# One transformer block on one core: loads on two queues, Wq transposes early, output buffers in turn, eleven numerator products, a new hand-off order

## The chip, the cores and the metric

The kernel runs on one core of one Trainium2 chip. The metric is the time of one execution on the device, in microseconds; the median of three runs of the kernel before is 277.59 us (277.17 to 278.16). One execution was also profiled: its own time is 276.56 us, and the span from its first to its last instruction is 274.8 us.

## The reference

The input x has 2048 rows of 640 values, in bfloat16. The block is an attention without a score matrix, followed by a gated product, each behind a layer norm and a residual.

```python
qkv = layernorm(x) @ wqkv                       # 640 x 1920; 32 heads of 20
pq, pk = q @ w_phi[head], k @ w_phi[head]       # 20 x 20 for each head
phi_q = concat(softmax(pq), softmax(-pq))       # 40 features a head; the same for phi_k
kv, z = phi_k^T v, sum over rows of phi_k       # one 40 x 20 block and 40 sums for each head
o = (phi_q kv) / (phi_q z + 1e-6)
h = x + o @ wo
g, u = layernorm(h) @ w_gate, layernorm(h) @ w_up   # 640 x 1536 each
out = h + (g * u) @ w_down                      # 1536 x 640
```

## The kernel before, in words

The 2048 rows are 16 tiles of 128 rows. All weights and all of x stay in the core's memory once loaded.

**What is computed in the beginning.** `Phi` is laid out as blocks (`Ph`). `w_phi` is folded into the K and Q weights: Wk is transposed by TensorE (`WT0..4`, line 391) and multiplied by `Phi` (`F1_0..4`, line 410). Wq is transposed by the DMA, straight from memory (`wqt0..4`, line 310: five transposes of 128x640), and multiplied by `Phi` (`F0_0..4`, line 410 again). A fold product of Wq needs all five transposes.

**For each row tile t.** Statistics of the row (`L1s`, `L1a`, lines 427 to 430), normalized rows (`xn`), their transpose (`xt`: by TensorE for tiles 0 to 3, line 461, by the DMA for the others, line 470). Then projections of ten 320-column products each: `V`, `K` and `Q` (line 483). `K` and `Q` go through two exponentials on ScalarE (`Kx`, `Qx`, line 495), a sum per head on VectorE (`Ks`, `Qs`, line 499), a reciprocal by ln and exp on ScalarE (`Kr`, `Ke`, lines 502 and 504) and a product on GpSimd (`Kn`, line 519, or `Qn`, line 550). `KV` (line 527) adds the tile to the sum over all rows. After all 16 `KV` the sums are masked (`KVe`), and for each tile follow the transposed features (`qT`, line 561), the numerators and denominators (`N`, line 575), the division (`dd`, `rd`, `o`, lines 586 to 591), the transpose of o (`oT`, line 595), the product with Wo (`O`, line 601), the residual (`h`, line 605), the second layer norm (`L2s`, `L2a`, `hc`) and its transpose (`hT`, line 628).

**The gated part** has row blocks of 256, 512, 512, 512 and 256 rows. `U` (line 643) is the product with the gate or up weights, `g` (line 648) moves the gate half from the accumulator, `u` (line 651) multiplies both, and `D` (line 662) is the product with the down weights. `y` (line 674) adds the residual, and `w` (line 676) writes the output.

**What sets the order.** Nothing is scheduled at run time. A table in the source, `PLAN` (lines 47 to 147), gives each operation a key, and where there is a choice an engine and a buffer slot; a planner outside the kernel wrote it from its own costs. `arrange` (line 685) sorts each engine's operations by the key, so an engine takes its operations in that order and waits at the first that is not ready. A semaphore wait of a DMA's issue also stands in that order. Loads and output writes are issued on SP's queue or on ScalarE's, by the second number of the entry; DMA transposes are always issued on SP.

**The loads before.** SP issues everything that the first tiles need, one after another: x0, w5, wk0, wk1, x1, wk2, x2, wk3, wk4, x3, wv1, wv0, wv2, x4, wv4, wv3, then x6 to x15. `PACE` (lines 307, 320 to 328 and 473) ties each of the five `wqt` to a transpose `xt` of tile 8 to 12, and all of Wo, Wd, Wgate and Wup to `xt15`: in `PLAN` they come at 27 to 51. Three of them, wg1, wu2 and wd0, are on ScalarE's queue.

**Other pieces that the change touches.** Ten warm-up products write one accumulator bank (lines 368 to 373). `N` uses eleven feature blocks of three heads (the last of two), into two banks that hold 16 heads each; block 5 has heads 15 to 17 and is cut in two, so there are twelve products. `out` has three buffers, but the plan gives slot 0 to nearly every `y`: at the end y14, y11, y10, y12 and y13 all have slot 0, and only y15_1 has slot 1.

Of the kernel before, what the change touches and what calls it, by code (L numbers as in the profile page):

```python
# [8 lines left out]
ALU = mybir.AluOpType  # L9
# [47 lines left out]
L1s5:11.357 L1a5:14.537 L1s6:13.607 L1a6:14.647 L1s7:12.177 L1a7:14.427 L1s8:19.637 L1a8:22.207 L1s9:16.397 L1a9:22.097 L1s10:14.757 L1a10:20.567
L1s11:15.577 L1a11:20.457 L1s12:25.657 L1a12:33.07 L1s13:30.22 L1a13:32.96 L1s14:29.4 L1a14:35.53 L1s15:33.18 L1a15:35.42 L1l0:4.311 L1e0:4.741
L1l1:8.905 L1e1:9.335 L1l2:10.717 L1e2:11.689 L1n2:12.199 L1n3:11.999 L1l4:14.996 L1e4:15.839 L1n4:16.349 L1n5:16.749 L1n6:16.149 L1n7:16.549
L1l8:23.514 L1e8:23.974 L1n8:24.884 L1n9:24.484 L1n10:24.684 L1n11:24.284 L1l12:35.85 L1e12:36.28 L1n12:37.279 L1n13:37.479 L1n14:36.879 L1n15:37.079  # L60
xn0:5.073::0 xt0:5.753::2 xte0:6.412 xn1:9.817::0 xt1:10.517::0 xte1:11.066 xn2:12.997::0 xt2:13.801::2 xte2:14.372 xn3:13.036:1:1 xt3:14.08::3
xte3:15.216 xn4:17.809:1:2 xt4:21.977 xn5:17.717::1 xt5:19.257 xn6:19.146:1:3 xt6:20.617 xn7:17.217::0 xt7:17.897 xn8:26.814:1:2 xt8:31.277
xn9:31.04::0 xt9:33.997 xn10:25.861:1:1 xt10:28.557 xn11:25.157::0 xt11:25.837 xn12:37.812::1 xt12:38.492 xn13:39.771:1:3 xt13:43.052 xn14:37.661:1:0
xt14:46.812 xn15:39.732::2 xt15:41.212 V0_0:9.115::2 V0_1:9.702 V0_2:10.245 V0_3:11.339 V0_4:11.611 Ve0:12.412::0 K0_0:8.004::4 K0_1:8.492 K0_2:9.973
K0_3:10.796 K0_4:11.067 Kx0_0:11.789::0 Kx0_1:13.749 Ks0:18.217::0 Kr0:20.483 Ke0:21.346 Kn0:21.706 KV0:30.148::6,7 V1_0:12.442::6 V1_1:12.714
V1_2:13.257 V1_3:13.529 V1_4:14.359 Ve1:16.562::1 K1_0:11.899::0 K1_1:12.171 K1_2:12.986 K1_3:14.631 K1_4:14.902 Kx1_0:15.939::1 Kx1_1:17.186
Ks1:20.677::1 Kr1:23.734 Ke1:24.698 Kn1:25.084 KV1:30.463 V2:16.564::2 Ve2:18.523::2 K2:15.206::4 Kx2_0:19.859::2 Kx2_1:20.723 Ks2:22.317::2
Kr2:24.848 Ke2:25.711 Kn2:27.443 KV2:32.137 V3:17.922::6 Ve3:28.648:1:6 K3:19.281::0 Kx3_0:21.496::3 Kx3_1:22.891 Ks3:23.737::3 Kr3:26.574 Ke3:27.527
Kn3:29.802 KV3:37.886 V4:24.714::0 Ve4:26.477:1:4 K4:27.431::0 Kx4_0:29.164::6 Kx4_1:30.411 Ks4:31.54::1 Kr4:33.14 Ke4:34.003 Kn4:34.52 KV4:38.201
V5:23.356::2 Ve5:27.677::5 K5:21.997::4 Kx5_0:24.074::4 Kx5_1:25.087 Ks5:27.228::0 Kr5:28.924 Ke5:31.658 Kn5:32.161 KV5:44.265 V6:28.789::2  # L70
Ve6:31.034::0 K6:26.073::4 Kx6_0:28.301::5 Kx6_1:29.788 Ks6:34::2 Kr6:35.61 Ke6:36.07 Kn6:37.679 KV6:44.581 V7:20.639::2 Ve7:22.267::3 K7:30.779::4
Kx7_0:32.407::0 Kx7_1:33.38 Ks7:35.64::0 Kr7:37.421 Ke7:39.621 Kn7:40.038 KV7:47.199 V8:36.527::0 Ve8:38.374::2 K8:35.169::4 Kx8_0:36.797::2
Kx8_1:38.997 Ks8:40.232::2 Kr8:42.181 Ke8:43.052 Kn8:44.756 KV8:48.873 V9:39.875::0 Ve9:41.652:1:4 K9:38.517::2 Kx9_0:40.724::3 Kx9_1:41.557
Ks9:42.403::3 Kr9:44.928 Ke9:46.895 Kn9:47.255 KV9:54.937 V10:42.907::2 Ve10:44.575:1:6 K10:41.233::4 Kx10_0:43.202::6 Kx10_1:44.305 Ks10:45.327::0
Kr10:47.045 Ke10:47.908 Kn10:49.614 KV10:56.611 V11:33.811::2 Ve11:37.06:1:1 K11:32.452::0 Kx11_0:34.153::1 Kx11_1:34.987 Ks11:38.312::1 Kr11:40.484
Ke11:41.347 Kn11:42.397 KV11:59.643 V12:55.253::0 Ve12:56.965:1:2 K12:45.526::2 Kx12_0:47.285::4 Kx12_1:48.118 Ks12:48.952::1 Kr12:50.6 Ke12:51.05
# [160 lines left out]
def build_graph():  # L237
# [66 lines left out]
    xload("sp", 6, 8, 5.8, also=["act"])  # L304


    PACE = {t: [] for t in range(NT)}

    def wqt(g, key):
        return G.op("sp", "wqt%d" % g, lambda e: e.dma_start_transpose(  # L310
# [589 lines left out]
```

## Time and profile before

| what | value |
|---|---|
| median of three runs | 277.59 us |
| the profiled execution's own time | 276.56 us |
| its span | 274.8 us |
| TensorE busy | 266.0 us, 97% of the span |
| VectorE, ScalarE, GpSimd busy | 172.3, 113.2 and 88.6 us |
| granted TensorE clock, mean | 0.999 |
| DMA, queue q1 (issued by SP) | 65888 packets, 26.15 MB, 44.8% of 16 engines |
| DMA, queue q10 (issued by ScalarE) | 688 packets, 1.28 MB, 1.9% |
| gated products, line 643 | 600 of them, 34% of the chain that ended last |
| projections, line 483 | 480 of them, 22% |

How to read it: busy time of TensorE counts a product until its result is out, so products that follow one another overlap in it; a row of a timeline such as "2.72 us for 20 products" gives the pace, 136 ns for 320 columns. The DMA share counts the time of packets on 16 engines. Idle time in front of an instruction is shown in brackets with what ended it.

### The profile page before, as it was taken

The page shows a single profiled execution, that of the slowest core. Times are in us where ns is not written, and L with a number is a line of the kernel's source. Part 1 is how long each engine was busy: PE and PEld are TensorE (multiplying, and loading weights), DVE is VectorE, ACT ScalarE, POOL GpSimd, SP SyncE. Part 2 cuts the span into 40 slices and gives each one's busy share as a digit, 9 for nine tenths or more (in the row PEclk, how much of TensorE's full clock was granted, in tenths as well). Part 3 has the DMA queues.
Part 4 walks back from the last instruction along what each step waited for, and adds up shares of the span by engine and source line. Part 5 has one row for each costly group of instructions (what it writes and reads, how often), then busy time and mean ns, then how long its engine had stood idle before and what let it go on. Part 6 is the DMA issues. An engine that isn't in the chain of part 4 may idle for free.

```text
span 274.8 us, 5227 instructions
## 1 busy us (share of the span) xinstructions
PE 266.0 (97%) x2119; PEld 176.7 (64%) x2119; DVE 172.3 (63%) x319; ACT 113.2 (41%) x240; POOL 88.6 (32%) x105
## 2 busy tenths in 40 slices
PE   7899999899999799999999999999999999999995
PEld 3676777677777587764455787665554467544773
DVE  5899999767789979987576337433365122323432
ACT  4899887678985444303242232003012310033000
POOL 7016999979998438240000000000000000000000
PEclk9999999999999999999999999999999999999999
DMA  6944758999689789867522100331002001100011
GB/s 167 317 144 95 98 110 174 302 294 341 141 147 176 146 141 186 163 74 160 52 47 49 26 0 2 84 50 48 25 2 48 0 0 50 52 0 2 24 48 57
DMA packets 66600, 27.77 MB, mean 101 GB/s; under 512 B 57744, under 2 KB 65296, under 8 KB 66576
## 3 DMA queue, kind: packets, MB, share of 16 engines
q1 hardware_dynamic: 65888, 26.15, 44.8%
q10 hardware_dynamic: 688, 1.28, 1.9%
q8 instruction: 17, 0.28, 0.4%
q14 instruction: 7, 0.06, 0.1%
HBM read 11.00 MB, written 2.62 MB: 50 GB/s over the span
## 4 chain that ended last, share of the span: by engine, by line
PE 84%; DMA 7%; DVE 4%; SPq 3%; issue 0%; DVEq 0%; ACT 0%
PE ps L643 34%; PE ps L483 22%; PE ps L662 17%; PE ps L601 7%; DMA xnT<-xn 3%; SPq L284 2%; PE ps L575 2%; DMA Wp<-in_A_wqkv_dram 2%; DMA scratch<-o 2%; DVE SR L499 2%; PE ps L527 1%; DMA out_dram<-Wp 1%; DVE o L591 1%; SPq L595 0%; DVE Wp L674 0%
## 5 line engine op out<-in xcount | busy, mean ns | idle before, releaser
L643 PE MATMUL ps<-xnT,Wgu 128*128 128x512 bf16 (+1 forms) x600 | 107.0, 336 | 1.2 <-DMA xnT<-xn 1.0
L643 PEld LDWEIGHTS ps<-xnT,Wgu 128*128 128x128 bf16 x600 | 58.0, 98 | 44.2 <-DVE ev L651 1.2
L648 ACT ACTIVATE gt<-ps 128x512 bf16<-128x512 f32 (+1 forms) x60 | 30.7, 512 | 101.9 <-PE ps L643 89.0
L483 PE MATMUL ps<-Wp,xnT 128*128 128x320 bf16 x480 | 69.0, 299 | 1.7 <-DMA xnT<-xn 1.3
L483 PEld LDWEIGHTS ps<-Wp,xnT 128*128 128x128 bf16 x480 | 45.2, 98 | 19.3 <-DMA xnT<-xn 1.8
L651 DVE TENSOR_TENSOR ev<-ps,gt 128x512 bf16<-128x512 f32 (+1 forms) x60 | 33.0, 577 | 37.6 <-PE ps L643 18.7
L662 PE MATMUL ps<-Wd,ev 128*128 128x320 bf16 (+2 forms) x396 | 53.2, 295 | 0.0
L499 DVE TENSOR_REDUCE SR<-ek 128x64 f32<-128x1280 bf16 x32 | 46.8, 1471 | 6.1 <-ACT ek L495 4.2
L495 ACT ACTIVATE ek<-ps 128x640 bf16<-128x640 f32 x64 | 43.3, 703 | 11.4 <-PE ps L483 10.1
L662 PEld LDWEIGHTS ps<-Wd,ev 128*128 128x128 bf16 x396 | 38.2, 98 | 14.9
L550 POOL TENSOR_TENSOR ph<-ek,SR 128x1200 bf16<-128x1200 bf16 x16 | 35.5, 2220 | 13.5 <-DMA scratch<-ph 7.4
L519 POOL TENSOR_TENSOR ek<-ek,SR 128x1280 bf16<-128x1280 bf16 x16 | 37.3, 2355 | 6.6 <-ACT SR L504 6.5
L674 DVE SCALAR_TENSOR_TENSOR Wp<-ps,rs,x_all 128x640 bf16<-128x640 f32 (+3 forms) x18 | 14.3, 805 | 35.5 <-PE ps L662 32.3
L615 POOL TENSOR_SCALAR ln<-mv 128x1 f32<-128x1 f32 x16 | 3.3, 209 | 87.2 <-DVE mv L614 87.2
L601 PE MATMUL ps<-Wo,scratch 128*128 128x320 bf16 x160 | 23.7, 299 | 0.2 <-DMA scratch<-o 0.2
L601 PEld LDWEIGHTS ps<-Wo,scratch 128*128 128x128 bf16 x160 | 15.3, 98 | 6.7 <-DVE ev L651 0.3
L605 DVE TENSOR_TENSOR x_all<-ps,x_all 128x640 bf16<-128x640 f32 x16 | 13.1, 816 | 3.7 <-PE ps L601 3.7
L624 ACT ACTIVATE xn<-x_all,mv 128x640 bf16<-128x640 bf16 x10 | 8.2, 825 | 16.5 <-DVE mv L614 16.5
L591 DVE TENSOR_TENSOR o<-ps,sm 128x640 bf16<-128x640 f32 x16 | 12.9, 814 | 1.5 <-DMA scratch<-o 1.0
L427 DVE BATCH_NORM_STATS2 st<-x_all 128x6 f32<-128x320 bf16 x16 | 7.7, 479 | 3.1 <-DMA x_all<-in_A_x_dram 3.0
L502 ACT ACTIVATE SR<-SR 128x64 f32<-128x64 f32 x32 | 8.1, 254 | 3.1 <-DVE SR L499 2.9
L575 PEld LDWEIGHTS ps<-KVm,scratch 128*128 128x128 bf16 x192 | 7.4, 98 | 2.9 <-DMA scratch<-ph 0.8
(54 smaller groups left out, 150.0 us busy)
## 6 DMA issues: line engine op xcount, KB each, us to landing
out_dram<-Wp SPq DMA_DIRECT2D x15, 160.0 KB, 1.8
x_all<-in_A_x_dram SPq DMA_DIRECT2D x6, 320.0 KB, 6.0
Wgu<-in_B_w_gate_dram SPq DMA_DIRECT2D x4, 384.0 KB, 7.5
Wgu<-in_B_w_up_dram SPq DMA_DIRECT2D x4, 384.0 KB, 8.5
Wd<-in_B_w_down_dram SPq DMA_DIRECT2D x3, 480.0 KB, 10.9
scratch<-in_A_wqkv_dram SPq DMA_DIRECT2D x5, 160.0 KB, 3.2
Wp<-in_A_wqkv_dram SPq DMA_DIRECT2D x5, 160.0 KB, 4.7
x_all<-in_A_x_dram SPq DMA_DIRECT2D x4, 160.0 KB, 3.4
```

The lines of the kernel that those rows point to most:

```text
L483: ins = e.matmul(pb(b, hb)[:, 0:320], lhsT=T["xnT"][:, NC - 1 - c, P * t:P * (t + 1)], rhs=T["Wp"][:, POS[kind], c, 320 * hb:320 * (hb + 1 ...
L495: G.op("act", "%sx%d_%d" % (nm, t, s), lambda e, s=s, b=b, ek=ek: e.activation(out=T["ek"][:, ek.slots[0], :].rearrange("p (b h s f) -> p ...
L499: G.op("dve", "%ss%d" % (nm, t), lambda e, ek=ek, sr=sr: e.tensor_reduce(out=T["SR"][:, sr.slots[0], 0, :], in_=T["ek"][:, ek.slots[0], :] ...
L519: G.op("pool", "Kn%d" % t, lambda e, ek=ek, sr=sr: e.tensor_tensor(out=T["ek"][:, ek.slots[0], :].rearrange("p (h f) -> p h f", f=DH), in0 ...
L550: e.tensor_tensor(out=o_[:, 0:10 * P].rearrange("p (g n) -> p g n", n=P)[:, :, 0:120].rearrange("p g (h f) -> p g h f", f=DH), in0=i_[:, 0 ...
L591: G.op("dve", "o%d" % t, lambda e, sm=sm, b=b, o=o: e.tensor_tensor(out=T["o"][:, o.slots[0], :].rearrange("p (b h d) -> p b h d", b=2, d= ...
L601: ins = e.matmul(pb(b, hb)[:, 0:320], lhsT=T["oT"][:, oT.slots[0], c, :], rhs=T["Wo"][:, c, 320 * hb:320 * (hb + 1)], start=(c == 0), stop ...
L643: ins = e.matmul(pb(b)[:, 0:n], lhsT=T["Wgu"][:, gu, c, P * ft:P * (ft + 1)], rhs=T["xnT"][:, NC - 1 - c, o0:o0 + n], start=(c == 0), stop ...
L648: G.op("act", "g%d_%d" % (bi, ft), lambda e, pg=pg, gt=gt, n=n: e.activation(out=T["gt"][:, gt.slots[0], 0:n], in_=pb(pg)[:, 0:n], func=AF ...
L651: o_ = G.op("dve", "u%d_%d" % (bi, ft), lambda e, pu=pu, gt=gt, hh=hh, ft=ft, n=n: e.tensor_tensor(out=T["hh"][:, hh.slots[0], ft, 0:n], i ...
L662: ins = e.matmul(pb(b, hb)[:, 0:w], lhsT=T["hh"][:, hh.slots[0], ft, P * tt:P * (tt + 1)], rhs=T["Wd"][:, ft, c0 + w * hb:c0 + w * (hb + 1 ...
L674: return e.scalar_tensor_tensor(out=o, in0=i0, scalar=T["rs2"][:, t:t + 1], in1=i1, op0=ALU.mult, op1=ALU.add)
```

## The change

- **Queues in the beginning.** ScalarE's queue now issues, ahead of its first arithmetic, x1, wk1, x12, wv4, x14, x8, x6, wv2, wu0, wd1, wd2 and wo0; then, between its first small operations, wu1, wg1, wo2, wd3, wg2, wg4, wg0, wd0 and wu2, and later wg3. SP issues w5, x0, wk0, x2, wk3, wk2, wk4, x3, wv1, wv0, wqt0, wv3, wqt4, x4, wqt1, wqt3, wqt2, x10, wu4 and wu3, and then the first transpose of a row tile.
- **`PACE` is gone.** The late weights and the `wqt` are no longer tied to an `xt`; their place comes from the table alone.
- **Order.** All five `F0` and the products Q0 to Q3 now stand right behind K3, V2, V3 and K2 on TensorE, ahead of KV0. In the kernel before, the first `F0` stood behind K10, and Q1 behind K13. The rest of the table is new too: with it `O14`, `N10`, `D0` and others change places, and Ph0 to Ph2 are all on GpSimd.
- **Buffers in turn.** The last outputs y14, y12, y11, y13, y10 and y15_1 have slots 0, 1, 2, 0, 1, 2; the buffers of `g`, `o` and others rotate likewise.
- **Numerators.** The two banks hold 18 and 14 heads, no block is cut, and `N` has eleven products instead of twelve. `dd`, `rd` and `o` work on 36 heads (720 columns) instead of 32 (640); the last four are not used.
- **Warm-up.** The first eight products write eight different banks.

```diff
-x0:0.7 w5:1.18:1 wk0:1.66:1 wv0:5.98:1 wk1:2.14 wv1:5.5 wk2:3.1:1 wv2:6.46:1 wk3:4.06 wv3:7.9 wk4:4.54:1 wv4:7.42:1 x1:2.62 x2:3.58 x3:5.02:1 x4:6.94
-x6:8.38 x8:9.34 x10:9.82 x12:10.3 x14:8.86 wqt0:32.637 wqt1:35.357 wqt2:29.917 wqt3:27.197 wqt4:39.852 wo0:44.412 wo2:45.852 wd0:45.168:1 wd1:51.052
+x0:1.18 w5:0.7:1 wk0:1.66:1 wv0:5.02:1 wk1:1.18:1 wv1:4.54 wk2:3.1:1 wv2:4.06 wk3:2.62 wv3:6.86 wk4:3.58:1 wv4:2.14 x1:0.7:1 x2:2.14 x3:4.06:1 x4:8.7
+x6:3.58:1 x8:3.1:1 x10:13.26 x12:1.66:1 x14:2.62:1 wqt0:5.5 wqt1:9.18 wqt2:11.9 wqt3:10.54 wqt4:7.34 wo0:5.98:1 wo2:7.96:1 wd0:13.577:1 wd1:5.02:1
+wd2:5.5:1 wd3:8.44:1 wg0:13.097:1 wu0:4.54:1 wg1:7.48:1 wu1:6.68:1 wg2:9.02:1 wu2:15:1 wg3:28.37:1 wu3:14.22 wg4:10.123:1 wu4:13.74 id0:0.9 gl0:1.2
...
     for g in range(NC):
-        PACE[8 + g].append(wqt(g, 10 * (8 + g) - 19))
-    PACE[15] += [wrows("wo", lambda: T["Wo"], "A_wo", wo_b[0:2], 0, 2, 328, 81), wrows("wo", lambda: T["Wo"], "A_wo", wo_b[2:5], 2, 5, 492, 81)]
+        wqt(g, 10 * (8 + g) - 19)
+    wrows("wo", lambda: T["Wo"], "A_wo", wo_b[0:2], 0, 2, 328, 41)
+    wrows("wo", lambda: T["Wo"], "A_wo", wo_b[2:5], 2, 5, 492, 44)
...
     for k in range(NWARM):
-        G.op("pe", "warm%d" % k, warm, 0.43 if k < 8 else 0.22, LT, [z_b], [wm_b], -90)
+        def warm(e, k=k):
+            o = T["PS"][:, 512 * k:512 * (k + 1)] if k < 8 else pb(wm_b)
+            return e.matmul(o, lhsT=T["zero"][:, 0:P], rhs=T["zero"][:, :], start=True, stop=True)
...
-            for o_ in PACE[t]:
-                o_.before.append(G.by["xt%d" % t])
...
             for g in range(NB):
-                for h0, h1 in [(3 * g, 3 * g + BH[g])] if g != 5 else [(15, 16), (16, 18)]:
-                    y = h0 // 16
-                    ins = e.matmul(pb(b, y)[:, 21 * (h0 - 16 * y):21 * (h1 - 16 * y)], lhsT=T["phT"][:, phT.slots[0], g, :],
+                y, h0, h1 = g // 6, 3 * g, 3 * g + BH[g]
+                ins = e.matmul(pb(b, y)[:, 21 * (h0 - 18 * y):21 * (h1 - 18 * y)], lhsT=T["phT"][:, phT.slots[0], g, :],
...
-            in1=smv(sm, 1).unsqueeze(3).to_broadcast([P, 2, 16, DH]), op=ALU.mult), dve_c(640, True), LD, [b, sm], [o], kk)
+            in1=smv(sm, 1).unsqueeze(3).to_broadcast([P, 2, 18, DH]), op=ALU.mult), dve_c(720, True), LD, [b, sm], [o], kk)
```

More of the change, by code (lines that the diff above doesn't have):

```diff
@@ L48 @@
 for _t in """
-x0:0.7 w5:1.18:1 wk0:1.66:1 wv0:5.98:1 wk1:2.14 wv1:5.5 wk2:3.1:1 wv2:6.46:1 wk3:4.06 wv3:7.9 wk4:4.54:1 wv4:7.42:1 x1:2.62 x2:3.58 x3:5.02:1 x4:6.94
-x6:8.38 x8:9.34 x10:9.82 x12:10.3 x14:8.86 wqt0:32.637 wqt1:35.357 wqt2:29.917 wqt3:27.197 wqt4:39.852 wo0:44.412 wo2:45.852 wd0:45.168:1 wd1:51.052
-wd2:50.092 wd3:46.332 wg0:42.572 wu0:49.132 wg1:42.572:1 wu1:44.892 wg2:49.612 wu2:43.825:1 wg3:48.652 wu3:48.172 wg4:50.572 wu4:45.372 id0:2.41
-gl0:0.7 eps:0.95 id1:2.93 gla0:3.77 glb0:4.21 gla4:2.19 glb4:3.33 gla1:1.97 glb1:3.55 gla2:4.43 glb2:4.85 gla3:2.71 glb3:3.99 va1:1.15 phz:6.025
@@ L57 @@
[L57 to L64, printed above, removed]
@@ new lines @@
+F1_4:11.437::2 Fe1_4:12.473:1 L1s0:4.903 L1a0:6.252 L1s1:3.993 L1a1:5.723 L1s2:6.804 L1a2:9.862 L1s3:12.089 L1a3:13.729 L1s4:21.009 L1a4:23.249
+L1s5:19.149 L1a5:20.899 L1s6:13.839 L1a6:15.479 L1s7:16.089 L1a7:19.969 L1s8:12.909 L1a8:39.144 L1s9:14.659 L1a9:39.034 L1s10:29.242 L1a10:41.174
+L1s11:32.092 L1a11:34.332 L1s12:7.624 L1a12:11.227 L1s13:18.329 L1a13:27.212 L1s14:25.641 L1a14:30.062 L1s15:20.079 L1a15:25.531 L1l0:7.26 L1e0:8.92
+L1l1:6.46 L1e1:7.16 L1l2:14.057 L1e2:14.9 L1n2:15.41 L1n3:15.21 L1l4:23.68 L1e4:24.673 L1n4:26.819 L1n5:27.219 L1n6:27.019 L1n7:26.619 L1l8:42.367
@@ new lines @@
+L1e8:43.211 L1n8:44.226 L1n9:44.626 L1n10:44.426 L1n11:44.826 L1l12:31.11 L1e12:32.817 L1n12:33.127 L1n13:33.527 L1n14:33.327 L1n15:33.727
+xn0:9.362::1 xt0:10.103::0 xte0:11.227 xn1:8.862::0 xt1:9.545::7 xte1:10.391:1 xn2:16.103:1:3 xt2:17.773::5 xte2:18.687 xn3:15.589::2 xt3:16.678::4
+xte3:17.44 xn4:27.322::0 xt4:28.002 xn5:27.657:1:1 xt5:29.362 xn6:36.573:1:0 xt6:37.902 xn7:30.172::2 xt7:30.852 xn8:46.761::2 xt8:48.462
+xn9:45.811:1:1 xt9:47.102 xn10:44.841::0 xt10:45.742 xn11:51.061::3 xt11:52.822 xn12:35.862::3 xt12:36.542 xn13:42.704::3 xt13:43.482 xn14:38.534::1
@@ L146 @@
+U4_10_0:161.931::5 U4_10_1:166.285::3 g4_10:162.747::1 u4_10:168.918 U4_11_0:162.477::4 U4_11_1:160.294::6 g4_11:163.293::0 u4_11:169.879
+D14_0:252.445::3 y14_0:255.975::0 w14_0:256.906 D15_0:186.473::7 y15_0:188.373::0 w15_0:188.971 D15_1:268.745::0 y15_1:270.005::2 w15_1:270.47
+D15_2:171.449::7 y15_2:172.974::0 w15_2:173.544
 """.split():
@@ L304, in build_graph @@
     xload("sp", 6, 8, 5.8, also=["act"])
-    PACE = {t: [] for t in range(NT)}
     def wqt(g, key):
@@ L366, in build_graph @@
     wm_b = Buf("pwarm", "psum")
-    def warm(e):
-        for _ in range(1):
-            ins = e.matmul(pb(wm_b)[:, 0:512], lhsT=T["zero"][:, 0:P], rhs=T["zero"][:, :], start=True, stop=True)
-        return ins
     for k in range(NWARM):
-        G.op("pe", "warm%d" % k, warm, 0.43 if k < 8 else 0.22, LT, [z_b], [wm_b], -90)
+        def warm(e, k=k):
+            o = T["PS"][:, 512 * k:512 * (k + 1)] if k < 8 else pb(wm_b)
+            return e.matmul(o, lhsT=T["zero"][:, 0:P], rhs=T["zero"][:, :], start=True, stop=True)
+        G.op("pe", "warm%d" % k, warm, 0.43 if k < 8 else 0.22, LT, [z_b], [] if k < 8 else [wm_b], -90,
+             before=[G.by["warm%d" % j] for j in range(min(k, 8))])
+    wall = [G.by["warm%d" % k] for k in range(8)]
     for k, (c0, c1) in enumerate(((0, 2), (2, 3), (3, 5))):
@@ L393, in wt @@
             return ins
-        G.op("pe", "WT%d" % i, wt, mm_c(*[P] * NC), LT, [wkn_b[i], id_b], [b], -90 + i)
+        G.op("pe", "WT%d" % i, wt, mm_c(*[P] * NC), LT, [wkn_b[i], id_b], [b], -90 + i, before=wall)
         evac("WTe%d" % i, lambda e, eng, i=i, b=b: copy(
@@ L464, in build_graph @@
             G.op("pe", "xt%d" % t, xt, mm_c(*[P] * 5), LT, [xb, id_b], [b], 10 * t - 20,
-                 before=[G.by["warm%d" % (NWARM - 1)]] if t == 0 else [])
+                 before=wall)
             evac("xte%d" % t, lambda e, eng, t=t, b=b: copy(
@@ L572, in nf @@
             for g in range(NB):
[L573 to L578 removed]
+                y, h0, h1 = g // 6, 3 * g, 3 * g + BH[g]
+                ins = e.matmul(pb(b, y)[:, 21 * (h0 - 18 * y):21 * (h1 - 18 * y)], lhsT=T["phT"][:, phT.slots[0], g, :],
+                               rhs=T["KVm"][:, h0:h1, :].rearrange("p h e -> p (h e)"),
+                               start=seen[y], stop=True, skip_group_check=True)
+                seen[y] = False
             return ins
[L580 removed]
+        G.op("pe", "N%d" % t, nf, mm_c(*[21 * n for n in BH]), LT, [phT] + kvm_b, [b], kk)
         def nv(b, lo, hi):
[L582 removed]
+            return pp(b, 0, 378).rearrange("p b (h e) -> p b h e", e=21)[:, :, :, lo:hi]
         sm = Buf("sm%d" % t, "sm")
```

187 lines of the change are left out of this document (90 added, 97 removed).

## The prediction

> **What bounds the kernel now.** I read the engines' busy time first, then the chain that ended last, then TensorE's timeline for the gaps in it.
>
> ```profile
> PE 266.0 (97%) x2119; PEld 176.7 (64%) x2119; DVE 172.3 (63%) x319; ACT 113.2 (41%) x240; POOL 88.6 (32%) x105
> ...
> PE 84%; DMA 7%; DVE 4%; SPq 3%; issue 0%; DVEq 0%; ACT 0%
> ```
>
> TensorE is the bound almost everywhere, so the order of its work is worth nothing in itself; only gaps count. These are all that its timeline shows behind the first 12 us (start, length, then in brackets the gap before it and what ended it):
>
> ```profile
> 12.97 2.62 PE L483 MATMUL ps<-Wp,xnT 128*128 128x320 bf16 x18 [0.42 <-DMA Wp<-in_A_wqkv_dram]
> ...
> 53.04 5.61 PE L483 MATMUL ps<-Wp,xnT 128*128 128x320 bf16 x40 [1.30 <-DMA xnT<-xn]
> ...
> 92.27 1.53 PE L601 MATMUL ps<-Wo,scratch 128*128 128x320 bf16 x10 [0.16 <-DMA scratch<-o]
> 94.08 0.89 PE L575 MATMUL ps<-KVm,scratch 128*128 128x63 bf16 x24 [0.28 <-DMA scratch<-ph]
> 96.01 9.45 PE L643 MATMUL ps<-xnT,Wgu 128*128 128x256 bf16 x85 [1.04 <-DMA xnT<-xn]
> ```
>
> Every one ends with a DMA: transfers decide this kernel. TensorE runs without a break from 15.99; the first six of the 116 products there belong to tile 1, so K2 starts at 15.99 + 6 x 0.136 = 16.8. The last product ends at 271.5. That is 254.7 us, less 2.8 us of gaps: 251.9 us of work from K2 on.
>
> **How two queues share the engines.** The change puts two long queues beside each other. The trace has that case once: a transpose xt13 on SP's queue q1 beside wd0 on ScalarE's q10. The DMA view of that stretch, 50.8 to 51.6 (packets, MB, share of 16 engines):
>
> ```profile
> q10 hardware_dynamic: 183, 0.23, 79.1%
> q1 hardware_dynamic: 180, 0.05, 25.7%
> ```
>
> The packets alternate, one for one, although one kind is five times as large. From the shares, a 1280-byte packet takes 79.1% x 0.8 x 16 / 183 = 55 ns of an engine and a 256-byte packet of a transpose 18 ns. Alone, one transpose is 640 such packets (673 with its signals from 18.6 to 22.0, 20 ns each): 40 for each engine, 0.8 us. Beside 1280-byte packets its 40 turns last 40 x 73 ns = 2.9 us, beside 3072-byte packets (125 ns, from the 272 packets and 99.8% of 61.5 to 63.4) 5.7 us. So a transpose gets a quarter of the engines' time or less.
>
> The Trainium skill, "DMA: Bandwidth & Descriptors", section "Queues, rings and completion order", says that each DMA engine goes round-robin over the queues that have work, by packet; its section "Issuing engines are not separate DMA queues" says that issuing from several engines saves only issue time. The trace agrees: 183 to 180. Those sections speak against this change. If each queue had half of the time instead, the Wq transposes would come much earlier; that is the first rival.
>
> **When Wq is there.** F0 needs all five `wqt`; the last on SP's queue is wqt2. Ahead of its end are, in packets for each of 16 engines (a 160 KB load has 8, x4 16, a transpose 40):
> - SP: w5, 640 packets of 40 bytes, 40 x 11 ns = 0.4 us (it passes among the 676 packets of 1.8 to 2.8); ten loads and x4, 96 x 60 ns = 5.8 (55 above; 776 packets in 91.8% of 6 to 9 give 57 with the signals, and the first 6 us are slower); five transposes, 200 x 19 ns = 3.8. In all 336 packets, 10.0 us.
> - ScalarE, all of its list but wg3: 232 packets of 1280 bytes = 13.9 us and 56 of 3072 bytes (wu0, wu1, wg1, wg2, wg4, wg0, wu2) = 7.0. In all 288 packets, 20.9 us. None of these waits for anything but operations of the first microseconds.
>
> 288 is less than 336, so turn by turn all of ScalarE's packets go ahead of wqt2's last. The first packets run at 1.9 us and a landing is told 0.8 us behind its last packet (xt13: last packets near 52.2, landed at 53.0): 1.9 + 10.0 + 20.9 + 0.8 = 33.6. The engines also pause: from 49.9 to 50.8 both queues had work and only 42 packets moved; 29.1 to 30.0 shows 25. I add two pauses of 1 us: **wqt2 lands at 35.5**, bounds 32.5 and 38.
>
> TensorE arrives earlier. wv3 is behind 160 packets of SP, with as many of ScalarE's, 6.0 + 10.1 us, so it lands near 1.9 + 16.1 + 0.8 = 18.8 (before, 12.93). Behind it stand 18 products of tiles 0 and 1, two transposes and K3, V2, V3, K2: 58 x 0.136 + 0.6 = 8.5, so F0 is reached at 27.3. It waits 8.2 us, and everything behind it waits too: Q0 to Q3, all later K and V, and on ScalarE and VectorE, which also run in order, the moves Fe0 of these products and what stands behind them. The late first tiles are hidden by this wait.
>
> **The sum.** Behind the start of F0 TensorE has the 251.9 us from above, less K2, V2, V3, K3 (40 x 0.136 = 5.4), less the numerators. Two `N` of twelve products take 0.71 us on the chain; two `KV` of eleven take 0.67; 16 x 0.02 = 0.3. Left: 246.2.
>
> A wait of 8 us also costs clock. In the last 2.8 us of the span the mean granted clock is 0.93, so it fell to a half 0.4 us before the end, 2.9 us behind the last product. In the beginning the ten warm-up products take 4.04 us, 404 ns each against 216 ns for 512 columns later. So 4 us at the half pace follow the wait: between 0 and 2.0 us lost, I take 1.7. The Trainium skill, "TensorE: Matmul & The Clock Gate", section "What's actually happening", gives an idle window of about 3.4 us for the fall and as long for the rise, which by its figure would be 1.7 too.
>
> Before the first U there are again waits for transposes of the attention: 1.48 us before, 0 to 2 now, I take 0.9. N adds to VectorE: `o` of 720 columns instead of 640, by the slope of line 651 (685 - 413 ns for 256) 85 ns each, beside TensorE's work and inside these 0.9.
>
> The end: y13 waited for the output in its only slot,
>
> ```profile
> 271.46 1.21 DVE L674 SCALAR_TENSOR_TENSOR Wp<-ps,rs,x_all 128x640 bf16<-128x640 f32 x2 [3.19 <-DMA out_dram<-Wp]
> ```
>
> so y15_1 ended at 272.67 though its product ended at 271.5. With slots in turn it ends 0.05 + 0.41 behind the last product, and 2.16 follow as before: 2.6 instead of 3.3, a gain of 0.7. The 1.30 at 51.7 goes too, since by then no loads are left; it is counted, because the 246.2 hold no gaps. Warm-up banks, the buffers of `g`, and Phi on GpSimd (0.7 us more of POOL ahead of F1) lie ahead of, or beside, longer things and count nothing; without the wait at F0 Phi could cost up to 1 us.
>
> 35.5 + 1.7 + 246.2 + 0.9 + 2.6 = **286.9 of span**, 12.1 more than 274.8. Upon 276.56 that is 288.7, and upon the median, which is 1.0 higher, 289.7; I say **289**.
>
> **Rivals.**
> 1. *Both queues get equal time, F0 is not starved* (not slower). SP's 10.0 us then end at 1.9 + 20 + 0.8 = 22.7, and TensorE, busy with K2, reaches F0 near 24.5: 24.5 + 246.2 + 0.9 + 2.6 = 274.2 of span, 276 to 277. The kernel is slower from the point where wqt2 lands later than 25.1. For it: a transpose in a stretch in which ScalarE's queue is empty moves in 0.8 us; the new order stands on it. Against it: 183 to 180.
> 2. *ScalarE is held by its own full queue.* SP's transpose at 49.65 took 4.66 us to issue with seven transfers ahead of it, 128 packets for an engine:
>
> ```profile
> 49.65 4.66 SPq L470 DMA_TRANSPOSE xnT<-xn  x1
> ```
>
>    ScalarE puts 240 packets ahead of L1e0 and of Fe1. If it must wait until 112 are gone, that is 1.9 + 7.2 of its own + 4.7 of SP's = 13.8. From L1e0 (4.58) to the first K product (9.14) pass 4.6 us now, so K starts at 18.4, and its 80 products and two transposes end at 29.9. If F0 is starved this is hidden; if it is not, 29.9 + 1 of clock + 246.2 + 0.9 + 2.6 = 280.6 of span, near 283.
> 3. *The change does more good than I see*: the waits ahead of U go as well. With rival 1 this gives 275.
>
> **Chances.** Forecast 0.72 (284 to 294), rival 2 alone 0.08 (280 to 285), rival 1 0.16 (275.5 to 279), rival 3 0.04. A measurement of this kernel can tell about 0.3% from no change, 0.8 us. Faster by more: 0.11, within: 0.07, slower by more: 0.82. The range reaches from rival 2 to the upper bounds of the landing (38), the clock and the waits: 280 to 294.
>
> **What would show it.** A gap of 5 us or more in front of the first 128x140 product of line 409 (410 before), ended by a DMA from in_A_wqkv_dram, at 32 to 38 us; a granted clock below 1 there; landings of the five `wqt` of 10 us and more where 3.5 is their median now; no gap near 50; the last y right behind its product. If wqt2 lands below 25 us the forecast is wrong at its first step. If F0 starts late but the time does not follow, TensorE's later work had slack that I do not see.

## The result, and the profile after

The kernel after takes 289.07 us in the median of six runs (287.83 to 292.04), the kernel before in the same series 277.38 (276.7 to 278.74): a ratio of 1.0427, 95% interval 1.0371 to 1.0482. It is slower, by about what was forecast (289). Its profiled execution took 288.41 us, with a span of 286.7 us, where 286.9 was worked out; the mean granted clock is 0.97. Executions more than 1.5% above the fastest of the same kernel are left out of the ratios, here and below.

From the page of the kernel after, the busy time and the chain that ended last:

```profile
PE 270.8 (94%) x2103; PEld 181.3 (63%) x2103; DVE 172.9 (60%) x320; ACT 111.1 (39%) x237; POOL 89.6 (31%) x107
...
PE 82%; DMA 8%; SPq 7%; DVE 2%; issue 1%; DVEq 0%
```

TensorE is busy 4.8 us longer with 16 products fewer: products at half the clock count longer. SPq, which issues SP's transfers, has 7% of the chain instead of 3%. TensorE's timeline after says where (start, length, gap in brackets):

```profile
15.49 0.71 PE L460 MATMUL ps<-ident,xn 128*128 128x128 bf16 x5 [1.90 <-DVE xn L451]
...
19.02 0.76 PE L409 MATMUL ps<-Phi,scratch 128*128 128x140 bf16 x6 [1.40 <-ACT Wp L251]
19.57 5.90 PE L480 MATMUL ps<-Wp,xnT 128*128 128x320 bf16 x34
...
26.68 5.60 PE L480 MATMUL ps<-Wp,xnT 128*128 128x320 bf16 x40
35.59 3.16 PE L409 MATMUL ps<-Phi,scratch 128*128 128x140 bf16 x30 [3.32 <-DMA scratch<-in_A_wqkv_dram]
...
105.02 1.53 PE L597 MATMUL ps<-Wo,scratch 128*128 128x320 bf16 x10 [1.20 <-DMA scratch<-o]
...
132.69 3.40 PE L639 MATMUL ps<-xnT,Wgu 128*128 128x512 bf16 x15 [0.56 <-DMA xnT<-xn]
```

F0 waits for the Wq transposes until 35.59 and 3.32 us long. The first K product (line 480) starts at 19.57; it was 9.14. The gap of 1.30 near 52 is gone. The chain of waits, in order of time, leads to F0 through SP's issues:

```profile
12.64 2.50 SPq L309
15.18 5.87 SPq L309
21.09 14.30 DMA scratch<-in_A_wqkv_dram
35.59 3.16 PE ps L409 x30
```

Line 309 issues the `wqt`. One issue lasted 5.87 us, where the first `wqt` took 1.26: I read this as a queue that was full, which no view shows directly. The last transpose, issued at 21.09, was told as landed at 35.39, 14.3 later. What the engines did meanwhile is in the DMA view of the kernel after, 28 to 30:

```profile
q10 hardware_dynamic: 266, 0.73, 91.5%
q1 hardware_dynamic: 267, 0.07, 15.0%
```

Equal numbers of packets, 266 to 267, and ScalarE's large ones have six times the time. (Equal numbers can't tell a turn of one packet from a turn of several.) The granted clock around the wait (start:end, then the busy times of PE, PEld, DVE, ACT and POOL, the clock as the first number behind them):

```profile
7.20:21.50 14.30, 8.48 (x64) 6.25 (x64) 9.30 (x24) 4.38 (x10) 0.00 (x0) 0.53 1.08 354
...
35.60:40.00 4.40, 4.40 (x40) 3.98 (x41) 3.01 (x8) 3.12 (x7) 0.74 (x1) 0.62 0.54 203
```

Two stretches at low clock: the first tiles, whose products came in pieces, and the 4.4 us behind the wait.

### The profile page after: what moved, and what is told of

Read it like the earlier page. It is cut to its first block, busy times and chain, and to the rows that moved or that the text cites. A ratio compares the mean times of both kernels' runs of the same rounds, so it can differ in the third digit from the quotient of the medians.

```text
span 286.7 us, 5169 instructions
## 1 busy us (share of the span) xinstructions
PE 270.8 (94%) x2103; PEld 181.3 (63%) x2103; DVE 172.9 (60%) x320; ACT 111.1 (39%) x237; POOL 89.6 (31%) x107
## 3 DMA queue, kind: packets, MB, share of 16 engines
q1 hardware_dynamic: 61488, 19.53, 35.5%
HBM read 11.00 MB, written 2.62 MB: 48 GB/s over the span
## 4 chain that ended last, share of the span: by engine, by line
PE 82%; DMA 8%; SPq 7%; DVE 2%; issue 1%; DVEq 0%
PE ps L639 36%; PE ps L480 18%; PE ps L658 17%; PE ps L597 6%; DMA scratch<-in_A_wqkv_dram 5%; SPq L309 5%; SPq L285 2%; PE ps L524 2%; DMA scratch<-o 2%; PE ps L571 2%; DMA xnT<-xn 1%; PE ps L409 1%; DVE SR L496 1%; DVE x_all L601 0%; DVE xn L619 0%
## 5 line engine op out<-in xcount | busy, mean ns | idle before, releaser
L480 PEld LDWEIGHTS ps<-Wp,xnT 128*128 128x128 bf16 x480 | 46.5, 99 | 17.9
L611 POOL TENSOR_SCALAR ln<-mv 128x1 f32<-128x1 f32 x16 | 3.4, 211 | 72.8 <-DVE mv L610 72.5
L620 ACT ACTIVATE xn<-x_all,mv 128x640 bf16<-128x640 bf16 x12 | 9.9, 825 | 12.4 <-DVE mv L610 12.3
L587 DVE TENSOR_TENSOR o<-ps,sm 128x720 bf16<-128x720 f32 x16 | 14.0, 887 | 0.3
L451 DVE TENSOR_SCALAR xn<-x_all,mv,rs 128x640 bf16<-128x640 bf16 x12 | 7.1, 588 | 7.2 <-ACT rs L437 4.4
L409 PE MATMUL ps<-Phi,scratch 128*128 128x140 bf16 (+1 forms) x60 | 6.7, 303 | 4.7 <-DMA scratch<-in_A_wqkv_dram 3.3
## 6 DMA issues: line engine op xcount, KB each, us to landing
Wgu<-in_B_w_gate_dram ACTq DMA_DIRECT2D x5, 384.0 KB, 11.5
```

What stands on the lines that cost most here:

```text
L480: ins = e.matmul(pb(b, hb)[:, 0:320], lhsT=T["xnT"][:, NC - 1 - c, P * t:P * (t + 1)], rhs=T["Wp"][:, POS[kind], c, 320 * hb:320 * (hb + 1 ...
```

## The experiments

All ratios are to the kernel before, run on the same chip. The span and what stands behind it in the table are from the one profiled execution, which can be a short or a long one of its kernel. "F0" is the start of its first product, "K" that of the first K product, "wqt2" the landing of the last Wq transpose.

| kernel | ratio (95%) | span | K | wqt2 | F0 |
|---|---|---|---|---|---|
| before | 1 | 274.8 | 9.14 | | |
| after | 1.043 (1.037 to 1.048) | 286.7 | 19.57 | 35.39 | 35.59 |
| e1_paced | 1.021 (1.011 to 1.031) | 280.4 | 15.78 | 20.81 | 27.20 |
| e2_dense | 1.046 (1.040 to 1.052) | 290.0 | 14.47 | 19.84 | 25.91 |
| e3_split | 1.029 (1.022 to 1.035) | 284.7 | 14.55 | 24.20 | 34.54 |
| e4_before_early | 1.040 (1.035 to 1.046) | 288.9 | 18.20 | | |
| e5_late_x | 1.020 (1.014 to 1.025) | 283.4 | 11.42 | 18.21 | 23.21 |
| e6_half_rows | 1.048 (1.042 to 1.055) | 289.5 | 25.70 | 25.88 | 38.33 |
| e7_before_slots | 0.999 (0.997 to 1.002) | 274.8 | | | |
| e8_before_slots_num | 0.998 (0.995 to 1.002) | 275.5 | | | |
| e9_late_x2 | 1.007 (1.004 to 1.011) | 279.1 | 12.26 | 18.27 | 23.70 |
| e10_one_queue | 1.029 (1.025 to 1.034) | 286.5 | 15.13 | 20.45 | 26.56 |
| e11_late_x3 | 0.995 (0.992 to 0.998) | 274.5 | 12.64 | 18.29 | 24.06 |

**e1_paced.** The late weights out of the beginning:

```diff
-wu0:4.54:1 wd1:5.02:1 wd2:5.5:1 wo0:5.98:1 wu1:6.68:1 wg1:7.48:1 wo2:7.96:1
-wd3:8.44:1 wg2:9.02:1 wg4:10.123:1 wg0:13.097:1 wd0:13.577:1 wu2:15:1 wg3:28.37:1
+wo0:41.05:1 wo2:43.45:1 wg0:45.85:1 wu0:48.25:1 wg1:50.65:1 wu1:53.05:1 wg2:55.45:1
+wu2:57.85:1 wg3:60.25:1 wg4:62.65:1 wd0:65.05:1 wd1:67.45:1 wd2:69.85:1 wd3:72.25:1
```

> The kernel after, with the fourteen late weight loads that ScalarE issues (wu0 to wg3: Wo, Wd, five of gate and up) moved behind the K and V products of the first tiles, one at a time between the plan's 41 and 73. Nothing else changes. Theory (turns): ScalarE's queue now holds only 96 packets for an engine instead of 288, so the last Wq transpose lands at 1.9 + 10.0 + 96 x 0.055 + 0.8 + 1 for a pause = 19 us instead of 35.4; TensorE reaches F0 at 24 to 25 without a wait; from there 246.8 us to the last product (248.5 of the kernel after less 1.7 of clock) and 2.6 of tail give a span of 274 to 275, a time of 275.5 to 277.5, the same as before. Rival A (the new order itself costs it: early Q, other covers): the landing moves as well, but the time stays above 284. Rival B (only ScalarE, held by its full queue, costs it): the same as the theory here; the run called e3_split tells them apart.

Wq landed at 20.81 (19 expected), F0 waited for it no more, and the profiled span fell by 6.3 us. Rival A (above 284) is not settled by this run: its four executions took 282.14, 284.06, 286.95 and 290.25 us, and the profiled one is the shortest; e11 settles it. Even that one stayed 5 to 6 us above the expectation: F0 began at 27.2 instead of 24 to 25, since K began only at 15.78, and behind it came waits of 1.60, 0.89 and 0.26 us for row tiles whose transposes met the paced weights. The first of them:

```profile
54.69 1.53 PE L481 MATMUL ps<-Wp,xnT 128*128 128x320 bf16 x10 [1.60 <-DMA xnT<-xn]
```

Its transpose, xt13, landed 7.89 us after its issue began; 2.6 is usual where one runs alone. I take both for the same sharing in other places; e5 tests it.

**e2_dense.** The fourteen loads at 27.04 to 27.30 on ScalarE, behind Fe0_4.

> As e1_paced, but the same fourteen loads stand together right behind the last move Fe0_4 of the Wq fold on ScalarE, so that they run beside the transposes of tiles 4 to 11 instead of beside those of Wq. Theory (turns): Wq lands at 19 as in e1_paced and F0 starts at 24 to 25. Then 200 packets of an engine, some 16.6 us, alternate with the transposes behind it: each of 40 packets lasts 2.9 to 5.7 us instead of 0.8, five or six of them get through in the 20 us after 27, and ScalarE is held until 88 of its packets are gone, near 36. TensorE waits 3 to 8 us for tile 4 or for ScalarE; span 277 to 283. If the two queues shared by time, each transpose would take 1.6 us, TensorE's 5.4 us for a tile would cover it, and only the held ScalarE could be seen: span 274 to 277.

The direction was right, the size not: 290.0. ScalarE's timeline and TensorE's:

```profile
40.19 0.92 ACT L450 ACTIVATE xn<-x_all,nb,rs 128x640 bf16<-128x640 bf16 x1 [10.62 <-issue]
```

```profile
42.50 1.32 PE L525 MATMUL ps<-ev,ek 128*128 128x63 bf16 x22 [8.70 <-ACT ek L493]
```

Issuing the fourteen loads kept ScalarE from 28.4 to 39.8: 10.62 us without arithmetic, and TensorE waited 8.70 for its exponentials. The expectation (held to 36, 3 to 8 us of waits) had this too small. xt4 took 10.85 us and landed at 40.76, only 1.7 us before TensorE went on, so this run does not show which of the two, the held ScalarE or the slow transpose, is the larger part.

**e3_split.** wu0, wd1, wd2, wo0, wu1 and wg1 behind Fe1_4, seven more between the next operations of ScalarE.

> The kernel after, with ScalarE's late weights still early, but behind its first arithmetic: six of them behind the move Fe1_4, seven more one at a time between the exponentials of the first two tiles. ScalarE so starts its first operations without a full queue. Theory (turns): the 192 packets of these loads still go ahead of the last Wq transpose, whose 200 packets are not served by then, so it lands at 33 to 36; K starts near 13 instead of 19.6, TensorE reaches F0 at 24 to 26 instead of 32.3, and waits 8 to 11 us instead of 3.3; span as in the kernel after, 285 to 288. Rival B (the held ScalarE is what costs): the first tiles come 5 to 6 us earlier and so does all else; span 280 to 282.

This one missed, by my own arithmetic. Behind Fe1_4 meant 14.76, and by then wv3 and wqt4 were through (landed at 15.14 and 15.67): SP had x4 and three transposes left, 136 packets, so that at most as many of ScalarE's 192 could go ahead of the last. It landed at 24.2 and starved nothing. ScalarE was held all the same, a little later. Its timeline:

```profile
19.69 6.99 ACTq L286 DMA_DIRECT2D Wgu<-in_B_w_gate_dram  x2
20.50 0.69 ACT L252 ACTIVATE ev<-ps 128x640 bf16<-128x640 f32 x1
26.72 0.70 ACT L252 ACTIVATE xnT<-ps 128x640 bf16<-128x640 bf16 x1 [5.54 <-issue]
```

The move of tile 3's transpose waited behind the issues, TensorE waited 5.87 us for it, and F0 began at 34.54, one us earlier than in the kernel after. So a held ScalarE, with Wq in time, brought F0 nearly as late as in the kernel after. The spans of its four executions, 284.7 to 287.1, lie where the theory put them (285 to 288), but by luck, since the late landing behind that figure did not come; rival B named the cause, and its price (280 to 282) was too low.

**e4_before_early.** The kernel before, with thirteen late weights first on ScalarE's queue (keys 0.71 to 0.95, their tie to xt15 removed).

> The kernel before, with thirteen of the late weight loads (all that the kernel after puts early on ScalarE's queue) issued first on ScalarE's queue; the Wq transposes stay where they are, at 27 to 51. Theory (turns, and a queue that holds its engine): SP's 16 first loads now alternate with 192 packets, so the last V weights land near 22 instead of 13; ScalarE must see 64 to 80 packets go before its first operation, near 12 instead of 4.6; the K products start near 16.7 instead of 9.1. All else follows by as much, less at most 1.5 us of waits that the empty queues save later: span 280 to 284. Rival (early weights cost only because Wq is needed early): the first tiles are hardly later, and the time is within 2 us of the kernel before.

Both steps came as told, and more: the last V weights landed at 22.81, and ScalarE's first operation ran at 13.62 (12 expected), K at 18.20 (16.7). Its timeline, and TensorE's:

```profile
13.62 0.29 ACT L436 ACTIVATE ln<-mv,eps 128x1 f32<-128x1 f32 x1 [11.55 <-issue]
```

```profile
22.85 2.62 PE L484 MATMUL ps<-Wp,xnT 128*128 128x320 bf16 x18 [1.40 <-DMA Wp<-in_A_wqkv_dram]
...
35.82 9.68 PE L484 MATMUL ps<-Wp,xnT 128*128 128x320 bf16 x70 [2.58 <-DMA xnT<-xn]
```

Early weights cost 14 us between the two profiled spans (12 us between the medians on one chip) even where Wq is not needed early. K's start accounts for 9.1 of the 14. Most of the rest is in TensorE's gaps behind it: they add up to 7.4 us (1.40 and 2.58 above, 1.05 and 1.10 later, the others below 0.8), against 3.2 in the kernel before. The range (280 to 284) was too low since it let waits fall by up to 1.5 us there; they grew by 4.2.

**e5_late_x.** As e1, the weights at 53.2 to 87, the statistics of tiles 8, 9 and 12 a few places later on VectorE, and

```diff
-x6:3.58:1 x8:3.1:1 x12:1.66:1 x14:2.62:1 wv3:6.86 x4:8.7
+x6:5.08 x8:5.6 x12:5.1 x14:12.0 wv3:5.04 x4:5.06
```

> As e1_paced, with two more moves: the fourteen late weights stand later still on ScalarE (the plan's 53 to 87, behind the last transpose of a row tile), and x6, x8, x12 and x14, which ScalarE's queue carried beside the first weights in e1_paced, go to SP's queue behind wv3 and between the Wq transposes; the statistics of tiles 8, 9 and 12 stand a few places later on VectorE. ScalarE issues only x1, wk1, wv4 and wv2 early. Theory (turns): in e1_paced the K weights still shared with 64 packets of those x loads: the last of them landed at 11.65 (8.62 in the kernel before) and K began at 15.78, half of it at the low clock. Now it is behind 48 packets of SP's and 32 of ScalarE's: 1.9 + 0.4 + 80 x 0.057 + 0.8 = 7.7; K starts at 10.5 to 11.5, and F0, 11.4 later, at 22 to 23, with the last Wq transpose at 18 to 20; the waits of 1.60, 0.89 and 0.26 us for row tiles go too. Span 22.5 + 247.3 + 1.7 of waits before and in U + 2.6 = 274 (273 to 276), 6 less than e1_paced, about the kernel before (274.8). Rival (the new order costs 5 us by itself, whatever is loaded when): span stays at 279 to 281.

The beginning came as worked out (K at 11.42, F0 at 23.21, wqt2 at 18.21), the end did not: 283.4. TensorE's timeline, and its clock:

```profile
26.35 1.24 PE L410 MATMUL ps<-Phi,scratch 128*128 128x140 bf16 x12 [2.03 <-ACT Wp L252]
...
93.59 2.85 PE L598 MATMUL ps<-Wo,scratch 128*128 128x320 bf16 x10 [4.48 <-DMA scratch<-o]
```

```profile
24.30:26.40 2.10, 0.07 (x2) 0.05 (x2) 2.10 (x4) 1.96 (x7) 1.30 (x1) 1.00 0.00 0
26.40:27.40 1.00, 1.00 (x13) 1.00 (x14) 1.00 (x5) 1.00 (x3) 1.00 (x1) 0.57 0.00 0
27.40:34.30 6.90, 6.90 (x49) 4.65 (x48) 5.93 (x11) 5.13 (x12) 4.92 (x7) 0.81 0.47 68
```

VectorE, busy from 15.4 to 28 with statistics, delayed ScalarE and so F0 by 2.03; that short gap also cost clock. Near 90 the weights wd0 to wd3 ran beside the transposes of `o`: oT0 took 9.23 us. The spans of its six executions go from 279.6 to 284.9 us, some in the rival's range (279 to 281) and some above it, so the times decide nothing. The gaps point to late transfers and to VectorE's list, and not to the order, which e9 and e11 test.

**e6_half_rows.** The kernel after, each of thirteen early weight loads cut into two of half the columns (shown for Wd; Wo, gate and up alike):

```diff
-    lambda k=k: T["B_wd"][3 * P * k:3 * P * (k + 1), :].rearrange("(f p) n -> p f n", p=P)
+for r, n0 in (("", 0), ("r", 320)):
+    lambda k=k, n0=n0: T["B_wd"][3 * P * k:3 * P * (k + 1), n0:n0 + 320].rearrange("(f p) n -> p f n", p=P)
```

> The kernel after, with each of thirteen early weight loads of ScalarE cut into two loads of half the columns: the same bytes in packets of 640 and 1536 bytes instead of 1280 and 3072, 480 packets for an engine on that queue instead of 288. Theory (one packet in turn, whatever its size): the last Wq transpose still has 336 packets of SP's, and 336 of ScalarE's go with them; they are now only part of the list. With 32 ns for 640 bytes and 65 ns for 1536 (estimates, on the line through 18 ns for 256, 55 for 1280 and 125 for 3072) they take 14.3 us instead of 20.9: it lands at 28.8 (27 to 32) instead of 35.4. The weights land later by as much. ScalarE is held longer by its queue, since more packets stand ahead of its first operations, so F0 need not start earlier: span 285 to 292. Rival C (the engines are full and serve bytes in the order of issue): the same bytes are ahead, it lands at 35 to 37.

The sharpest test of the first step. Same bytes in all, smaller packets on the *other* queue, and wqt2 landed at 25.88 instead of 35.39. Rival C (35 to 37) is out. Up to 25.1 the DMA view counts 5664 packets of SP's and 5312 of ScalarE's, with 4.86 MB of ScalarE's ahead of the landing; up to 34.6 in the kernel after it is 7.51 MB. But it also came earlier than the expected 28.8 (27 to 32); the part on the prediction says why. The view of 18 to 20:

```profile
q10 hardware_dynamic: 594, 0.36, 58.3%
q1 hardware_dynamic: 587, 0.34, 55.0%
```

Again in equal numbers, at 58.3% x 2 x 16 / 594 = 31 ns a packet (32 estimated). The kernel was no faster: ScalarE, held by a longer list, let K begin at 25.70, and F0 followed at 38.33 with Wq long there.

**e7_before_slots, e8_before_slots_num.** The kernel before with

```diff
-y11_0:255.829::0 y10_0:259.089::0 y13_0:265.609::0 y15_1:266.599::1
+y11_0:255.829::1 y10_0:259.089::2 y13_0:265.609::1 y15_1:266.599::2
```

and, in e8, the eleven numerators with their banks and the warm-up banks as well.

> The kernel before, with the last outputs y14, y11, y10, y12, y13 and y15_1 in slots 0, 1, 2, 0, 1, 2 instead of 0, 0, 0, 0, 0, 1; nothing else. Theory: y13 no longer waits for the write of y12, so the last y ends 0.46 us behind the last product instead of 1.17: 0.7 us less (0.4 to 0.9), a ratio of 0.9975. Rival: the writes queue behind one another at the end, and nothing is gained.

> As e7_before_slots, with the numerators in eleven products as well (18 and 14 heads in the two banks; o of 720 columns; the first warm-up products in eight banks). Theory: 16 products of 0.02 us less on TensorE, 0.3 us; the longer o on VectorE is hidden or costs up to 0.5 in the waits before U. Together with the slots 1.0 us less than the kernel before (0.5 to 1.2), a ratio of 0.9965. Rival: the longer division delays the transposes of o, and the waits before U grow by what the products save: 0.7 us less, as e7_before_slots.

In the trace of e7 the last y stands right behind its product, as in the kernel after:

```profile
271.38 1.41 DVE L675 SCALAR_TENSOR_TENSOR Wp<-ps,rs,x_all 128x640 bf16<-128x640 f32 x2 [2.38 <-PE ps L663]
```

It ends 0.52 us behind the last product (272.27), 1.15 in the kernel before: 0.6 of the 0.7 is there. The times can't tell either from no change: both intervals hold 1. The 0.3 of the numerators stays unmeasured.

**e9_late_x2, e11_late_x3.** As e5, with the weights at 53.2 to 72.7 (e9) and 57.2 to 72.8 (e11), and the statistics of tiles 8 and 9 at 35.3 and 38.45.

> As e5_late_x, with two moves that its trace points to: the fourteen late weights stand at the plan's 53 to 73, 1.5 apart, in front of the transposes of the attention instead of among them, and the statistics of tiles 8 and 9 stand at 35 and 38 on VectorE, which was busy without a break from 15.4 to 28 there. Nothing else differs from the kernel after but the places of these loads and of the statistics of tile 12. Theory (the new order costs nothing of its own; what it lost went to transfers that shared the engines and to engines behind them): the 2.03 us in the middle of F0 fall to 0.5, the clock loss behind it (1.5) goes, and of the waits of 1.38 and 4.48 near 88 and 93 about 1.2 stay: span 283.4 - 1.5 - 1.5 - 4.7 = 275.7 (274 to 278), within 1.5 us of the kernel before. Rival (the order costs by itself): 280 or more.

> As e9_late_x2, with the fourteen late weights at the plan's 57 to 73, 1.2 apart, so that none is issued before the last transpose of a row tile, xt11, is done: in e9_late_x2 xt11 shared with wo0 and wo2, took 8.56 us, and TensorE waited 3.14 for it. Theory: xt11 takes 2.6 us again, the wait of 3.14 and some 1.3 us of clock behind it go, and nothing else needs a transpose before 76; span 279.1 - 4.4 = 274.7 (273.5 to 277), level with the kernel before (ratio 0.99 to 1.003). Rival: the weights, now denser, hold ScalarE or meet the first transposes of the attention near 80, and a wait of 2 to 4 us comes there: span 277 to 279, as e9_late_x2.

e9 took 279.1 in its profile (275.7 expected, 274 to 278): the old waits went, but wo0 and wo2 now met xt11. Its TensorE timeline and the DMA view of 56 to 62:

```profile
62.64 7.01 PE L481 MATMUL ps<-Wp,xnT 128*128 128x320 bf16 x40 [3.14 <-DMA xnT<-xn]
```

```profile
q10 hardware_dynamic: 697, 0.92, 83.0%
q1 hardware_dynamic: 1391, 0.34, 31.8%
```

ScalarE's packets have 83% of the engines there; xt11 landed 8.56 us after its issue began. Moved by 3 us, in e11, it took 4.57 and TensorE waited for it no more. These are all the gaps of e11 from F0 on:

```profile
25.71 0.81 PE L410 MATMUL ps<-Phi,scratch 128*128 128x140 bf16 x12 [0.53 <-ACT Wp L252]
...
44.40 1.53 PE L481 MATMUL ps<-Wp,xnT 128*128 128x320 bf16 x10 [0.22 <-ACT ek L493]
...
92.99 1.53 PE L598 MATMUL ps<-Wo,scratch 128*128 128x320 bf16 x10 [0.82 <-DMA scratch<-o]
98.15 11.08 PE L640 MATMUL ps<-xnT,Wgu 128*128 128x256 bf16 x100 [0.25 <-issue]
```

Span 274.5 (274.7 expected), ratio 0.995 (0.992 to 0.998): half a percent below the kernel before, little but clear of 1, and far below the kernel after. It has the order, the buffers and the numerators of the change; only the places of loads and of three tiles' statistics differ. So the order itself costs nothing, and the 4.3% of the kernel after lie in those places.

**e10_one_queue.** The thirteen weights on SP's queue behind x10.

> The kernel after, with the thirteen early weight loads of ScalarE on SP's queue instead, right behind the last Wq transpose and x10: as many bytes in the beginning, but one behind the other on one queue, and ScalarE issues only its first eight loads. Theory (turns between queues, and a held ScalarE, are what costs): the last Wq transpose lands at 21 as in e1_paced, ScalarE is free, F0 starts at 27; the weights then move until 39, and xt4, behind them on SP, lands near 40, when TensorE needs it near 36: a wait of 4 to 5 us for tile 4 and 1 to 1.5 of clock behind it. The later waits for row tiles of e1_paced (2.75 us) do not come. Span 280.4 + 4.5 + 1.3 - 2.75 = 283.5 (281 to 285), 3 less than the kernel after. Rival (early weights cost the same on any queue): F0 waits as in the kernel after, 286 to 288.

As told up to F0 (wqt2 at 20.45, F0 at 26.56), which the rival did not allow, but xt4 landed at 42.22, not 40, and TensorE waited for it:

```profile
42.26 2.85 PE L481 MATMUL ps<-Wp,xnT 128*128 128x320 bf16 x10 [7.13 <-DMA xnT<-xn]
```

The granted clock behind this was 0.50. The profiled span of 286.5 is the longest of four; the other three are 283.3, 283.8 and 284.9, inside the expected range (281 to 285). So the forecast of the time held in three of four, with a longer wait than the 4 to 5 us told. One queue moves the wait to the next transfer behind the weights; it does not remove it.

## Why the prediction was right, step by step

- **Turns between the queues, by packets: right.** 266 to 267 in the kernel after, 594 to 587 with half the packet size, and a landing that followed the count and not the bytes (e6).
- **wqt2 at 35.5: measured 35.39.** The Trainium skill, "DMA: Bandwidth & Descriptors", section "Queues, rings and completion order", has the engines go round-robin by packet; the trace agrees, 266 to 267, and the rival of equal time (22.7) is out. That it came out to 0.1 us is partly luck. The DMA view of 1.9 to 34.6 gives ScalarE's packets 70.6% and SP's 36.6% of that stretch: 23.1 and 12.0 us, where the sum had 20.9 and 10.0. The two shares make over 100%, so packets of the two queues overlap on the engines, and the sum has no overlap. It has two pauses of 1 us instead; the trace shows one such stretch (nine packets from 24.8 to 25.9) and shorter ones. In e6, whose expected landing took all of this over, no such stretch shows up in the view, and wqt2 came 2.9 us before the 28.8.
- **F0 reached at 27.3, a wait of 8.2: wrong in size.** wv3 landed at 17.83 (18.8), but TensorE ended K2 at 32.28 and waited 3.32. The step took rival 2 as an alternative; it happened at the same time. ScalarE's first operation ran at 9.91 (5.88 in e3, with eight loads ahead of it instead of twelve), its next issues lasted up to 2.62 us, and K began at 19.57 (18.4 in that rival). The loads are not the reason: the last K weights landed at 10.83, and at 10.93 in e3, where K began 5 us earlier. It stayed hidden since F0 waited anyway. But its price was too small: with Wq in time, F0 would have begun at 32.3, not 29.9, since K began 1.2 us later and its products took 1.2 us longer, the first ones at a clock of 0.5 (rival 2 has 1 us for clock). e3 and e6 show it bounding by itself.
- **Clock behind the wait, 1.7: right.** 4.4 us at a mean of 0.62 lose 1.67.
- **246.2 us of work from F0 on: 1.1 too much.** The last product ends at 284.12; 284.12 - 35.59 - 1.67 - 1.76 of gaps = 245.1. The same remainder in e11, with the same products, is 271.92 - 24.06 - 1.82 = 246.0; why the two differ is open.
- **Waits before the first U, 0.9: too small.** 1.20 for `oT2`'s transpose before the first U, as told in kind, and 0.56 for a transpose of the second layer norm at 132, which no step had: 1.76.
- **Tail of 2.6, a gain of 0.7: right in the trace.** 286.7 - 284.12 = 2.6; e7 shows 0.63 of it alone, below what its times can tell.
- **The signs.** All five `wqt` took 10.3 to 17.1 us from issue to landing (10 and more); no gap near 50; the last y behind its product. The gap ahead of F0 was told as 5 us or more and is 3.32, for the reason above.
- **Sum.** 35.59 + 1.67 + 245.1 + 1.76 + 2.6 = 286.7. As 245.1 is what the other terms leave, this sum closes by itself; the errors of 246.2 and 0.9 nearly cancel, and that the total is off by only 0.2 us is luck.

What the prediction did not see is how little of the loss hangs on Wq alone: 3.3 us of wait and 1.7 of clock, 5.0 of the 11.9 us of span. F0 comes at 35.59 here and at 24.06 in e11, and by the estimate of 32.3 above most of these 11.5 us would be there with Wq in time. The landing and the total came out as forecast because the late Wq still ended last, and hid the rest. Behind its late transposes stood the held ScalarE (e3, e6), behind that the first weights sharing with x loads (e1), and any later place beside a transpose cost again (e5, e9). Each removal showed the next.

## What to carry to other kernels

Before a load is moved to a second queue, count the packets that run beside each transfer on the path, not the bytes: here a transfer of small packets got through one packet for each large one. Count too what stands behind the issue on its engine, since many loads in a row held it for 5 to 12 us here. The place that cost nothing was a stretch in which TensorE awaited no transpose (57 to 73 in e11).

## What the runs showed of the hardware that was not expected

- Cutting the packets of one queue in half brought a transfer of the other queue 9.5 us forward (e6), although no byte was taken away: 4.86 MB of the other queue went ahead of it instead of 7.51.
- A gap of 2.03 us in TensorE's work was enough for the clock to fall (0.57 in the next microsecond, 0.81 over the 6.9 behind it, e5); gaps of 1.60 and 0.89 us in e1 were followed by 1.00, and so were longer ones of 2.58 us in e4 (35.8 to 39.0) and 2.50 in e2 (51.7 to 55.0). So the length of a gap alone does not decide it. The Trainium skill, "TensorE: Matmul & The Clock Gate", section "What's actually happening", gives an idle window of about 3.4 us that runs freely. The fall with the gap of 7.13 us agrees with that, and the one with 3.32 lies at its edge; the one with 2.03 us does not fit, and no run here shows why.
- An engine that issues many loads in a row stands still meanwhile: 10.62 us without arithmetic on ScalarE in e2, 11.55 in e4, 5.54 in e3, and 5.87 in one issue on SP in the kernel after. That a full queue holds it is the reading; no view shows how full a queue is.
